# Attention and a two-product MLP in one kernel: reordering the start of the software pipeline

## The chip, the cores and the metric

The kernel runs on one core of a Trainium2 chip. The metric is the device time of one execution in microseconds. The kernel before was run 13 times: the median is 257.85 us, the runs lie between 256.0 and 263.9 us. One execution was recorded by the hardware profiler; its own time is 257.47 us.

The engines are named as in the profile: PE is TensorE (PEld its weight loads), DVE is VectorE, ACT is ScalarE, POOL is GpSimd, SP is SyncE. POOL, SP and ACT also issue DMA transfers. Each engine works through its instructions in the order in which the program emits them, and waits where an operand isn't there yet.

## The reference

Inputs are q, k and v of shape (4, 8, 768, 64) in float32, and two weight matrices of 512 x 2048 and 2048 x 512. Attention is causal with a scale of 1/8. Of the eight heads, 0, 2 and 6 ("retrieval" heads) see all earlier tokens; the others ("stream" heads) see the first four tokens (the sink) and a window of the last 64:

```python
in_win = (rel >= 0) & (rel < int(window))
stream_keep = causal & (is_sink | in_win)
mask = np.where(retr[0, :, 0, 0, None, None], full_mask, stream_mask)
...
a = a / (np.sum(a, axis=-1, keepdims=True) + 1e-09)
attn_out = np.matmul(a, v)
```

The result is laid out as 3072 tokens of 512 features, and then

```python
h = x @ w_in
g = np.maximum(0.01 * h, h)
return (g @ w_out).astype(np.float32)
```

## The kernel before

**Chunks.** The tokens are cut into eight chunks of 384 (`CH`), two for each of the four batches: chunk n is half n % 2 of batch n // 2. For each chunk there are three pieces of work: attention n, product 1 of n (`in_slots`, x times w_in, sixteen ticks of four matmuls and one Prelu on ACT), and product 2 of n (`out_slots`, sixteen parts, 48 matmuls). Each is a list of Python closures; `run` emits a list, `merge` interleaves two lists evenly. The order in which the closures run is the program order of every engine. There is no planner; the order is written out by hand at the bottom of the kernel (lines 517 to 581).

**The steady state.** From chunk 2 on, the stage of chunk n interleaves product 1 of n, product 2 of n - 1 and attention n + 1 (lines 567 to 581). Before that, attention 0 runs alone, then product 1 of chunk 0 with the preparation of chunk 1 between its last ticks, then attention 1 merged with the last two ticks and product 2 of chunk 0 (line 557), then products 1 and 2 of chunk 1 merged with attention 2 (line 564).

**Loads.** `load(n)` issues the K, Q and V transfers of chunk n on POOL, in that order, three or six transfers each, with the cast to bf16 in the transfer. From chunk 2 on, K goes into one of two zero-padded buffers `kz[n % 2]` (line 86); the zeros between the heads are written once, by `zeros_k` on DVE (line 136). The weights w_in and w_out are loaded on POOL too, in quarters, between the loads of chunks 0, 1 and 2.

**K and Q transposed.** Attention needs K and Q with the features on the partitions. For chunk 0 `prep_first` and for chunk 1 `prep_pair` do it with PE transposes through PSUM. From chunk 2 on `prep_dma(n)` issues six DMA transposes on SP (lines 236 and 238): K and Q in turn, for each third of the chunk. A score of the first head needs all three thirds of Q.

**V shifted by half a tile.** The window of a stream head spans two tiles of 64 tokens, so V is needed a second time shifted by 64 rows, in `vb`. `v_shift(n)` makes it with two DMA copies (lines 182 and 183), on ACT's queue unless another is given; it must wait for chunk n's V. For chunk 0 `v_shift_pe` does it with matmuls.

**Sinks.** `sink_keys` copies the first four keys of the stream heads to `ksink` on DVE; `sink_values(b)` writes the first four value rows to `vs`, whose last column holds ones for the softmax sum.

**Attention in slots.** A unit is one score group (scores on PE, exp on ACT, mask on DVE), and its product with V follows `LAG` slots later. When both heads of a pair are done, `finish` adds the sinks and normalises on DVE (lines 413 and 415), and `XLAG` slots later `x_t` transposes the result on PE (line 421) and ACT copies it into `xt`, the input of product 1.

**PSUM.** Eight banks are shared by tag: two "ph" (product 1), two "psS" (scores), two "po" (attention output), one "py" (product 2), one "pt" (transposes). A tile of a tag waits until the last user of that bank is done.

**Queues.** The SP order before is: K of chunk 0; V shift 1; transposes of chunk 2; output stores of chunk 0; V shifts 2 and 3; transposes of chunk 3; output stores of chunk 1; transposes of chunks 4 and 5; output stores of chunk 2; and so on. V shifts 4 to 7 are on ACT, at the end of a stage.

Of the kernel before, what the change touches and what calls it, by code (L numbers as in the profile page):

```python
# [21 lines left out]
def kernel(  # L22
# [34 lines left out]
    def bank(tag, shape, dtype):  # L57
        return ps.tile(shape, dtype, name=tag, tag=tag, bufs=BANKS[tag])
# [98 lines left out]
    def late_constants():  # L157

        nc.vector.tensor_copy(shift[:, 0, 0:64], ident[:, 64:128])
        nc.vector.tensor_copy(shift[:, 1, 64:128], ident[:, 0:64])  # L160
        nc.vector.tensor_copy(m_win0[:, 1:], spread(m_w[:], 5, 64))
        nc.vector.tensor_copy(m_win0[:, 0, :], m_caus[:, 0:64])
        nc.vector.memset(m_win0[0:NS, 1, :], 1.0)
        for h in range(H):
            if IS_RETR[h]:
                nc.vector.memset(m_h[:, h : h + 1], 0.0)
        for i in range(2):
            nc.vector.tensor_copy(vs[i][:, :, D], m_h[:])

    def sink_values(b):  # L170
        m = m_h[:, 1:H].rearrange("p (h o) -> p h o", o=1).to_broadcast([128, H - 1, D])
        nc.vector.tensor_tensor(vs[b % 2][:, 1:H, 0:D], spread(sv[:, b, :], H - 1, D), m, op=ALU.mult)

# [25 lines left out]
    def sink_keys(n, p, hh):  # L199
        b, c = divmod(n, 2)  # L200
        h = 2 * p + hh
        if c == 0 and not IS_RETR[h]:
            r = slice(64 * hh, 64 * hh + 64)
            nc.vector.tensor_copy(ksink[b % 2][r, p, NS * h : NS * h + NS], kt[b % 2][r, p, hh, 0:NS])
# [35 lines left out]
    def prep_first():  # L240

        k0 = stage["k"].rearrange("p h (g d) -> p g h d", g=3)
        qts[0] = rot.tile([128, 4, CH], BF16, name="qt", tag="qt", bufs=2)
        nc.vector.tensor_copy(cast["k", 0][:, :, 0:4], k0[:, :, 0:4])
        nc.scalar.activation(out=cast["k", 0][:, :, 4:8], in_=k0[:, :, 4:8], func=ACTF.Copy)
        pts = {}
        for nm, half, tag in (("k", 0, "pt"), ("k", 1, "py"), ("q", 0, "po"), ("q", 1, "po")):
            pt = pts[nm, half] = bank(tag, [128, 2, 4, 128], BF16)
            if nm == "q":
                continue  # L250
            for e in range(2):
                p = 2 * half + e
                for g in range(3):
                    nc.tensor.transpose(pt[:, e, g, :], cast[nm, 0][:, g, 2 * p : 2 * p + 2, :], ident[:])
        for g in range(3):
            for p in range(4):
                nc.tensor.transpose(pts["q", p // 2][:, p % 2, g, :], cast["q", 0][:, g, 2 * p : 2 * p + 2, :], ident[:])
        tok = lambda ap: ap.rearrange("p e (t g) -> p e t g", g=3)

        def k_rows(half, hh, act=False):  # L260
            ps2 = slice(2 * half, 2 * half + 2)
            r = slice(64 * hh, 64 * hh + 64)
            src = pts["k", half][r, :, 0:3, :].rearrange("p e g t -> p e t g")
            dst = tok(kt[0][r, ps2, hh, 0:CH])
            if act:
                nc.scalar.activation(out=dst, in_=src, func=ACTF.Copy)
            else:
                nc.vector.tensor_copy(dst, src)

        def q_rows(half):  # L270
            return (qts[0][:, 2 * half : 2 * half + 2, :].rearrange("p e (g t) -> p e g t", g=3),
                    pts["q", half][:, :, 0:3, :])

        k_rows(0, 0)
        k_rows(0, 1)
        k_rows(1, 0, True)
        k_rows(1, 1)
        late_constants()
        d, r = q_rows(0)
        nc.scalar.activation(out=d, in_=r, func=ACTF.Copy)  # L280
        d, r = q_rows(1)
        nc.vector.tensor_copy(d, r)
        for h in range(H):
            sink_keys(0, h // 2, h % 2)
        sink_values(0)


    xts = {}
    ats_i = [0]

    class Attention:
        def __init__(self, n, score_tags=("psS",), po_tags=("po", "po", "po", "po")):
            self.n = n
            self.b, self.c = divmod(n, 2)
            self.i = self.b % 2
            xts[n] = rot.tile([128, 4, CH], BF16, name="xt", tag="xt", bufs=2)
            self.po = {}
            self.tags = score_tags
            self.po_tags = po_tags
            self.sc = 0  # L300
            self.sink_lo = 128 if self.c == 0 else 0
            self.units = {h: (self.retr(h) if IS_RETR[h] else self.stream(h)) for h in range(H)}
# [118 lines left out]
                nc.tensor.transpose(pt[:, 0, j, :], xs[:, j], ident[:])  # L421
            nc.scalar.activation(out=xts[self.n][:, p, :], in_=pt[:, 0, 0:3, :], func=ACTF.Copy)  # L422

        def slots(self, extra=(), order=range(H), extra_at=None, LAG=2, XLAG=2, sink_after=None):

            extra = list(extra)
            units = []
            seen = set()
            for h in order:
                if seen == (sink_after or {0, 1}) or (2 in seen and h == 1 and not sink_after):  # L430
                    units.append((self.sink, None, None))
                seen.add(h)
                units += self.units[h]
            sink_at = [j for j, u in enumerate(units) if u[1] is None][0]
            last = {p: max([sink_at] + [j for j, u in enumerate(units) if u[2] == p]) for p in range(4)}
            r, box = [], {}
            if extra and extra_at is None:
                r.append(extra.pop(0))
            for t in range(len(units) + LAG + XLAG):
                def slot(t=t):  # L440
                    for p in range(4):
                        if t == last[p] + LAG + XLAG:
                            self.x_t(p, box[p])
                    if t < len(units):
                        units[t][0]()
                    if 0 <= t - LAG < len(units):
                        if units[t - LAG][1]:
                            units[t - LAG][1]()
                        for p in range(4):
                            if t - LAG == last[p]:  # L450
                                box[p] = self.finish(p)
                r.append(slot)
                if extra and t in (extra_at or [last[p] + LAG + XLAG + 1 for p in range(4)]):
                    r.append(extra.pop(0))
            return r + extra
# [2 lines left out]
    gs = {}  # L458
    py = {}

    def in_slots(n):
        def tick(t):
            if t == 0:
                gs[n] = rot.tile([128, NG, CH], BF16, name="g", tag="g", bufs=2)
            ph = bank("ph", [128, 512], FP32)
            for g in range(KG):
                nc.tensor.matmul(ph[:, 0:CH], lhsT=w_in_bf[:, g, 128 * t : 128 * t + 128],  # L467
                                 rhs=xts[n][:, g, :], start=(g == 0), stop=(g == KG - 1))
            nc.scalar.activation(out=gs[n][:, t, :], in_=ph[:, 0:CH], func=ACTF.Prelu, alpha=0.01)  # L469

        return [lambda t=t: tick(t) for t in range(NG)]
# [27 lines left out]
    def run(*lists):  # L499
        for l in lists:  # L500
            for f in l:
                f()
# [32 lines left out]
    for i in range(4):  # L535
        load_w("out", i)
    prep_first()
    a0 = Attention(0, ("psS", "ph")).slots(order=[0, 2, 1, 3, 4, 5, 6, 7], LAG=4, XLAG=3, sink_after={0, 2})
    run(a0[0:8])
    v_shift_pe()  # L540
    run(a0[8:])
    zeros(0, 1)
    nc.vector.memset(ksink[1][:], 0.0)
    zeros_k(0)
    zeros_k(1)
    load(2)
    in0 = in_slots(0)
    run(in0[0:10])
    for p in range(4):
        prep_pair(1, p, ("py", "pt")[p % 2])  # L550
        run(in0[10 + p : 11 + p])
    v_shift(1, nc.sync)
    prep_dma(2)
    load(3)

    a1 = Attention(1, po_tags=("po", "po", "po", "ph")).slots(order=[0, 2, 6, 1, 3, 4, 5, 7])
    run(merge(in0[14:] + out_slots(0), a1))
    v_shift(2, nc.sync)
    v_shift(3, nc.sync)
    load(4)  # L560
    prep_dma(3)
    for h in range(H):
        sink_keys(2, h // 2, h % 2)
    run(merge(in_slots(1) + out_slots(1, ("py", "ph", "py")), Attention(2).slots()))
# [2 lines left out]
    for n in range(2, NCH):  # L567
        a = []
        if n + 3 < NCH:
            load(n + 3)  # L570
        if n + 2 < NCH:
            prep_dma(n + 2)
        if n + 1 < NCH:
            a = Attention(n + 1).slots()
        run(merge(merge(in_slots(n), outs) if outs else in_slots(n), a))
        if n + 2 < NCH:
            v_shift(n + 2)
            for h in range(H):
                sink_keys(n + 2, h // 2, h % 2)
        outs = out_slots(n) if n + 1 < NCH else out_slots(n, ("psS", "psS", "py"), True)  # L580
# [36 lines left out]
```

## Time and profile before

| what | us |
|---|---|
| median of 13 runs | 257.85 |
| profiled execution, its own time | 257.47 |
| span of the profile, first to last instruction | 255.8 |
| PE busy | 228.1 |
| ACT busy | 137.4 |
| DVE busy | 86.8 |
| POOL busy | 80.4 |
| first matmul of product 1, chunk 0 | 20.7 |
| first matmul of product 1, chunk 1 | 58.3 |
| first score of attention 3 | 91.0 |

The profile is a page and a trace that answers questions. The page gives the busy time of each engine, and the span in 40 slices with a digit for the busy tenths; the row PEclk is the clock that TensorE was granted. The waits list who stood still for whom: in total, how many times, the longest. The chain of waits is followed back from the last instruction, at each step to what released it. The timeline gives instructions in order of time (start, length, engine, line, what was written from what), with the idle time before them and what ended it in brackets. A table of stretches gives the busy time of each engine between two moments, with instruction counts in brackets. "DMA qt<-qb" is the transfer that writes `qt` from `qb`; a row of SPq or POOL with DMA in it is the issue of a transfer, not its landing.

### The profile page before, as it was taken

What the parts mean: (1) busy time and instruction counts of PE and PEld (TensorE: products, weight loads), DVE (VectorE), ACT (ScalarE), POOL (GpSimd) and SP (SyncE); (2) the same over time, 40 slices, a digit from 0 to 9 for tenths busy, and PEclk for the clock granted to TensorE, in tenths of its full rate; (3) what the DMA queues carried; (4) which work ended last, traced back from release to release, by engine and by line L of the source; (5) the groups of instructions that cost most, each with busy time, mean ns of one, the idle gap of its engine ahead of it and who ended that gap; (6) DMA issues with size and microseconds to landing.
All of it is one profiled execution on the core that took longest, in us unless ns stands there. A gap on an engine that the chain in (4) does not pass through costs nothing.

```text
span 255.8 us, 5001 instructions
## 1 busy us (share of the span) xinstructions
PE 228.1 (89%) x1984; PEld 137.9 (54%) x2012; DVE 86.8 (34%) x248; ACT 137.4 (54%) x297; POOL 80.4 (31%) x109
## 2 busy tenths in 40 slices
PE   1778866982999999998999999999999999999994
PEld 0464543561566556654665566655665566555543
DVE  6986331272123423333342224333431242211111
ACT  3575463541585279854665676665656577433300
POOL 8983824965491375286640000000000000000000
PEclk9999999997699999999999999999999999999999
DMA  9999999999999999999993971097103100111012
GB/s 161 114 205 179 168 233 174 125 142 172 214 155 141 134 212 160 149 135 177 176 168 71 117 148 44 0 147 163 44 0 107 41 11 32 41 42 43 8 74 85
DMA packets 110971, 30.14 MB, mean 118 GB/s; under 512 B 101732, under 2 KB 107108, under 8 KB 110948
## 3 DMA queue, kind: packets, MB, share of 16 engines
q0 software_dynamic: 76272, 13.24, 71.5%
q1 hardware_dynamic: 33936, 15.23, 32.6%
q10 hardware_dynamic: 740, 1.35, 2.6%
q8 instruction: 16, 0.26, 0.5%
q14 instruction: 7, 0.06, 0.1%
HBM read 27.28 MB, written 6.29 MB: 131 GB/s over the span
## 4 chain that ended last, share of the span: by engine, by line
PE 57%; DMA 28%; POOL 6%; SPq 4%; issue 2%; DVE 1%; ACT 0%; POOLq 0%
PE ph L467 23%; PE py L480 20%; DMA w_out_bf<-in_moe_w_out_dram 6%; DMA qt<-qb 6%; DMA w_in_bf<-in_moe_w_in_dram 5%; PE po L309 4%; PE psS L342 4%; PE psS L480 3%; DMA kz<-in_k_dram 3%; DMA va<-in_v_dram 3%; DMA vb<-va 3%; DMA kt<-kz 3%; SPq L236 3%; POOL va L93 2%; PE psS L378 1%
## 5 line engine op out<-in xcount | busy, mean ns | idle before, releaser
L467 PE MATMUL ph<-xt,w_in_bf 128*128 128x384 bf16 x512 | 103.9, 330 | 0.1
L469 ACT ACTIVATE g<-ph 128x384 bf16<-128x384 f32 x128 | 62.9, 491 | 49.1 <-PE ph L467 48.5
L480 PE MATMUL py<-w_out_bf,g 128*128 128x512 bf16 (+1 forms) x310 | 83.1, 373 | 5.7 <-DMA w_out_bf<-in_moe_w_out_dram 3.8
L467 PEld LDWEIGHTS <-w_in_bf 128*128 128x128 bf16 x512 | 45.6, 98 | 27.6 <-issue 2.8
L480 PEld LDWEIGHTS <-g 128*128 128x128 bf16 x400 | 36.4, 97 | 32.2 <-issue 5.4
L347 ACT ACTIVATE at<-psS 128x384 bf16<-128x384 f32 x81 | 38.6, 491 | 23.4 <-PE psS L342 19.7
L86 POOL DMA_DIRECT2D kz<-in_k_dram x36 | 27.0, 763 | 34.0 <-DMA kt<-kz 20.0
L342 PE MATMUL psS<-qt,kt 128*128 128x384 bf16 (+2 forms) x104 | 26.6, 299 | 4.9 <-DMA qt<-qb 4.7
L485 DVE COPY o<-py 128x512 f32<-128x512 f32 (+1 forms) x21 | 14.3, 679 | 39.6 <-PE py L480 37.6
L93 POOL DMA_DIRECT2D qb<-in_q_dram x24 | 21.3, 902 | 8.2 <-DMA w_out_bf<-in_moe_w_out_dram 1.9
L93 POOL DMA_DIRECT2D va<-in_v_dram x24 | 21.2, 907 | 7.2 <-DMA w_in_bf<-in_moe_w_in_dram 4.6
L422 ACT ACTIVATE xt<-pt 128x384 bf16<-128x384 bf16 x32 | 15.7, 489 | 14.5 <-PE pt L421 14.0
L383 ACT ACTIVATE ats<-psS 128x384 bf16<-128x384 f32 x38 | 18.5, 494 | 8.1 <-PE psS L378 8.1
L353 DVE TENSOR_TENSOR at<-at,m_caus 128x128 bf16<-128x128 bf16 x24 | 5.4, 224 | 50.7 <-ACT at L347 50.6
L309 PE MATMUL po<-va,at 128*128 128x65 bf16 x237 | 20.2, 195 | 0.2 <-DVE at L353 0.2
L309 PEld LDWEIGHTS <-at 128*128 128x128 bf16 x252 | 16.2, 99 | 5.8 <-DVE at L353 0.7
L342 PEld LDWEIGHTS <-kt 128*128 128x128 bf16 x108 | 10.5, 101 | 15.3 <-issue 7.9
L415 DVE TENSOR_TENSOR xs<-po,linv 128x384 bf16<-128x384 f32 x31 | 17.3, 557 | 1.1
L378 PEld LDWEIGHTS <-kt 128*128 128x128 bf16 x240 | 12.0, 99 | 6.2 <-issue 0.5
L309 PEld LDWEIGHTS <-ats 128*128 128x128 bf16 x240 | 11.8, 97 | 6.1 <-DMA vb<-va 1.3
L309 PE MATMUL po<-va,ats 128*128 128x65 bf16 x137 | 13.2, 194 | 0.5 <-DVE xs L415 0.4
L421 PE MATMUL pt<-ident,xs 128*128 128x128 bf16 x96 | 10.6, 219 | 3.2 <-DVE xs L415 2.0
(90 smaller groups left out, 157.7 us busy)
## 6 DMA issues: line engine op xcount, KB each, us to landing
out_dram<-o SPq DMA_DIRECT2D x23, 256.0 KB, 2.3
qb<-in_q_dram POOLq DMA_DIRECT2D x24, 128.0 KB, 6.7
va<-in_v_dram POOLq DMA_DIRECT2D x24, 128.0 KB, 8.0
kz<-in_k_dram POOLq DMA_DIRECT2D x36, 64.0 KB, 8.4
w_in_bf<-in_moe_w_in_dram POOLq DMA_DIRECT2D x4, 512.0 KB, 8.1
w_out_bf<-in_moe_w_out_dram POOLq DMA_DIRECT2D x4, 512.0 KB, 12.1
vb<-va SPq DMA_DIRECT2D x4, 195.0 KB, 6.9
vb<-va ACTq DMA_DIRECT2D x4, 195.0 KB, 3.1
```

Source lines behind the costliest of these rows:

```text
L86: nc.gpsimd.dma_start(out=kz[n % 2][:, g, hh::2, D * hh : D * hh + D], in_=nat[nm][b, c, :, hh::2, g])
L93: nc.gpsimd.dma_start(out=o, in_=nat[nm][b, c, :, :, g])
L309: nc.tensor.matmul(o, lhsT=lhsT, rhs=rhs, start=first, stop=False, skip_group_check=True)
L342: nc.tensor.matmul(s[:, off : off + w], lhsT=kt[i][:, p, hh, 128 * kj : 128 * kj + 128], rhs=qts[n][:, p, lo:CH], start=(j == 0), stop=(j ...
L347: nc.scalar.activation(out=a[:, 0:off], in_=s[:, 0:off], func=ACTF.Exp, scale=SM)
L378: nc.tensor.matmul(s[:, 64 * m : 64 * m + 64], lhsT=kt[i][:, p, hh, k0 : k0 + 128], rhs=qts[n][:, p, 64 * m : 64 * m + 64], start=(m == 0) ...
L383: nc.scalar.activation(out=av_, in_=s[:, 0:CH].rearrange("p (j e f) -> p j e f", j=3, e=2), func=ACTF.Exp, scale=SM)
L415: nc.vector.tensor_tensor(xs[:], po[:, :, :, 0:D], linv.to_broadcast([128, 3, 2, D]), op=ALU.mult)
L422: nc.scalar.activation(out=xts[self.n][:, p, :], in_=pt[:, 0, 0:3, :], func=ACTF.Copy)
L467: nc.tensor.matmul(ph[:, 0:CH], lhsT=w_in_bf[:, g, 128 * t : 128 * t + 128], rhs=xts[n][:, g, :], start=(g == 0), stop=(g == KG - 1))
L469: nc.scalar.activation(out=gs[n][:, t, :], in_=ph[:, 0:CH], func=ACTF.Prelu, alpha=0.01)
L480: nc.tensor.matmul(py[n][:, 0 : c1 - c0], lhsT=gs[n][:, ng, 128 * tt : 128 * tt + 128], rhs=w_out_bf[:, ng, c0:c1], start=(ng == 0), stop= ...
```

## The change

- Attention 1 is split: its first eight slots are merged with the last five ticks of product 1 of chunk 0, the rest with product 2 of chunk 0. For that the preparation of chunk 1 moves from behind tick 10 to behind tick 7.
- Product 1 of chunk 0 takes its PSUM banks in turn from "ph" and "psS".
- `zeros_k(1)` moves from before the load of chunk 2 to behind attention 1, and V shift 2 and `load(3)` follow it there. Since `load(3)` writes K into `kz[1]`, it waits for these memsets.
- On SP the transposes of chunk 3 now stand ahead of V shift 3.
- V shifts 4 to 7 go to SP, each directly behind the transposes of the same chunk, instead of to ACT at the end of the stage.
- `XLAG` is 3 instead of 2 by default. Attention 0 takes two banks in turn for the transposes of its result.
- In the first attention, `sink_keys` stands ahead of the constants, `sink_values(0)` behind the first six slots, the PE shift of V two slots earlier, and the ones column of `vs` is written by `sink_values` for each batch.

```diff
@@ sink_values, prep_first
-        for i in range(2):
-            nc.vector.tensor_copy(vs[i][:, :, D], m_h[:])
     def sink_values(b):
+        nc.vector.tensor_copy(vs[b % 2][:, :, D], m_h[:])
...
+        for h in range(H):
+            sink_keys(0, h // 2, h % 2)
         late_constants()
...
-        for h in range(H):
-            sink_keys(0, h // 2, h % 2)
-        sink_values(0)
@@ Attention
-        def __init__(self, n, score_tags=("psS",), po_tags=("po", "po", "po", "po")):
+        def __init__(self, n, score_tags=("psS",), po_tags=("po", "po", "po", "po"), x_tags=("pt",)):
-        def slots(self, extra=(), order=range(H), extra_at=None, LAG=2, XLAG=2, sink_after=None):
+        def slots(self, extra=(), order=range(H), extra_at=None, LAG=2, XLAG=3, sink_after=None):
-                            self.x_t(p, box[p])
+                            self.x_t(p, box[p], self.x_tags[p % len(self.x_tags)])
@@ in_slots
-            ph = bank("ph", [128, 512], FP32)
+            ph = bank(tags[t % len(tags)], [128, 512], FP32)
@@ the order of the work
-    a0 = Attention(0, ("psS", "ph")).slots(order=[0, 2, 1, 3, 4, 5, 6, 7], LAG=4, XLAG=3, sink_after={0, 2})
-    run(a0[0:8])
+    a0 = Attention(0, ("psS", "ph"), x_tags=("pt", "py")).slots(order=[0, 2, 1, 3, 4, 5, 6, 7], LAG=4, XLAG=3, sink_after={0, 2})
+    run(a0[0:6])
+    sink_values(0)
     v_shift_pe()
-    run(a0[8:])
+    run(a0[6:])
     zeros(0, 1)
     nc.vector.memset(ksink[1][:], 0.0)
     zeros_k(0)
-    zeros_k(1)
     load(2)
-    in0 = in_slots(0)
-    run(in0[0:10])
+    in0 = in_slots(0, ("ph", "psS"))
+    run(in0[0:7])
     for p in range(4):
         prep_pair(1, p, ("py", "pt")[p % 2])
-        run(in0[10 + p : 11 + p])
+        run(in0[7 + p : 8 + p])
     v_shift(1, nc.sync)
     prep_dma(2)
+    a1 = Attention(1, po_tags=("po", "po", "po", "ph")).slots(order=[0, 2, 6, 1, 3, 4, 5, 7])
+    run(merge(in0[11:], a1[:8]) + merge(out_slots(0), a1[8:]))
+    zeros_k(1)
+    v_shift(2, nc.sync)
     load(3)
-    a1 = Attention(1, po_tags=("po", "po", "po", "ph")).slots(order=[0, 2, 6, 1, 3, 4, 5, 7])
-    run(merge(in0[14:] + out_slots(0), a1))
-    v_shift(2, nc.sync)
-    v_shift(3, nc.sync)
     load(4)
     prep_dma(3)
+    v_shift(3, nc.sync)
...
             prep_dma(n + 2)
+            v_shift(n + 2, nc.sync)
...
         if n + 2 < NCH:
-            v_shift(n + 2)
```

More of the change, by code (lines that the diff above doesn't have):

```diff
@@ L299, in __init__ @@
             self.po_tags = po_tags
+            self.x_tags = x_tags
             self.sc = 0
@@ L459, with in_slots @@
     py = {}
-    def in_slots(n):
+    def in_slots(n, tags=("ph",)):
         def tick(t):
```

## The prediction

> **What bounds the kernel now.** I read the page first, then the waits of TensorE, then the stretches and the timeline around the longest of them.
>
> ```profile
> span 255.8 us, 5001 instructions
> PE 228.1 (89%) x1984; PEld 137.9 (54%) x2012; DVE 86.8 (34%) x248; ACT 137.4 (54%) x297; POOL 80.4 (31%) x109
> PEclk9999999997699999999999999999999999999999
> ```
>
> TensorE is the bound: 27.7 us of the span are not PE time, and the clock dips once, near 60 us. The waits of PE (in total, times, longest) say where it stands still:
>
> ```profile
> PE psS L342 <- DMA qt<-qb: 4.7, 1, 4.7
> PE py L480 <- DMA w_out_bf<-in_moe_w_out_dram: 3.8, 3, 1.9
> PE po L309 <- DMA vb<-va: 1.1, 1, 1.1
> PE py L214 <- DMA qb<-in_q_dram: 0.6, 1, 0.6
> ```
>
> The largest single one is attention 2's first score (L342), which needs the last transposed Q of chunk 2. The table of stretches (first column us, then PE, PEld, DVE, ACT, POOL, PEclk, DMA, GB/s) shows what it costs:
>
> ```profile
> 58.26:63.75 5.49, 0.81 (x6) 0.32 (x5) 1.33 (x6) 0.75 (x2) 3.45 (x5) 0.78 1.68 185
> 63.75:68.17 4.42, 4.42 (x15) 2.12 (x16) 0.52 (x2) 1.85 (x4) 0.75 (x2) 0.50 1.75 249
> 68.17:91.04 22.87, 22.57 (x203) 13.48 (x204) 7.60 (x21) 12.21 (x27) 11.15 (x14) 1.00 1.97 152
> ```
>
> 4.68 us of standstill and then 4.42 us at half clock, another 2.2 us of work lost. Why the transpose was late is in the timeline:
>
> ```profile
> 48.13 3.76 POOL L86 DMA_DIRECT2D kz<-in_k_dram  x5
> 54.09 1.76 POOL L93 DMA_DIRECT2D qb<-in_q_dram  x2 [1.12 <-DMA va<-in_v_dram]
> 55.06 1.33 SPq L238 DMA_TRANSPOSE qt<-qb  x1
> ...
> 59.61 0.47 SPq L182 DMA_DIRECT2D vb<-va  x1
> ...
> 71.17 0.46 SPq L182 DMA_DIRECT2D vb<-va  x1
> 72.29 0.46 SPq L183 DMA_DIRECT2D vb<-va  x1
> 72.85 1.79 SPq L236 DMA_TRANSPOSE kt<-kz  x1
> ```
>
> The last transpose of chunk 2 is issued at 55.06 and in the chain of waits lands 8.55 us later, while POOL has chunk 3's K loads (48.13) and Q loads (54.09) in flight. Six transposes with no load beside them take 12.2 us from first issue to last landing (138.69 to 150.86, the last one 2.9 us); here they take 19.5. Chunk 3's own transposes wait on SP until 72.85, behind the V shift of chunk 3 (71.17), which waits for the V load.
>
> **The change, part by part.** The sum is made against the profiled execution: 257.47 us, 1.7 around a span of 255.8; it lies 0.4 under the median of 257.85.
>
> *Prologue.* Sink keys ahead of the constants, `sink_values(0)` after six slots, a second bank for the X transposes, four banks for product 1: DVE work is reordered ahead of the first mask (sink values cost 0.63 us, the two ones-column copies 0.40), and gaps of 0.21, 0.44, 0.40 and 0.88 us before product 1 shrink. I estimate product 1 starting about 0.8 us earlier than 20.71. I cost this at nothing: all of it ends at w_out, whose last quarter lands at 43.1 (28.57 plus 14.5), whatever PE does; the POOL order before it does not change. Without that cover it would be a gain of 0.8. The per-batch ones copy (about 0.2 us of DVE, three times) hides beside 15 us of ACT and PE work per stage; uncovered it costs 0.6.
>
> *Preps of chunk 1 after seven ticks instead of ten.* This puts a wait on PE. K of chunk 1 lands at 24.6, 25.5 and 26.5 (issue 12.65, 13.53, 14.39 plus 11.9 to 12.1), the last Q at 29.1 (17.93 plus 11.2), and PE would be there at 19.9 + 7 x 0.67 = 24.6. So it drips transposes until 29.2, with all of PE's stream queued behind:
>
> ```profile
> 29.19 0.23 PE L214 MATMUL py<-ident,qb 128*128 128x128 bf16 x1 [0.63 <-DMA qb<-in_q_dram]
> ```
>
> Afterwards three more ticks (1.95 us) and four more attention slots (four scores and their products, 1.0) have to fit before w_out's last quarter. From 29.2 to 43.15 PE was busy 10.14 of 13.95 us, so 3.8 are free and 2.95 are used. Net: 1.0 us of attention 1 moves ahead of 43.15, and the stage's end goes from 58.26 to about 57.0 (XLAG 3 gives the other 0.2; the 0.58 wait for the single X bank at 57.66 stays).
>
> [...] In the trace the clock halved about 2.3 us after the last matmul (0.78 over 5.49 us is 2.4 us at half). [...] By the row of before (clock 1.00 with a 0.76 us wait there) nothing is lost. [...]
>
> *Chunk 3's loads held.* `zeros_k(1)` now stands on DVE behind the last copy of product 2 of chunk 0, and the K loads wait for it; K is first in the load, so Q, V and all later loads on POOL queue behind. No trace shows transposes of chunk 2 without that load. The bounds: the last one lands 2.5 to 6.9 us after its issue in the rows without loads (2.5, 2.9, 3.7, 6.9) and 8.55 in the row of before. V of chunk 2 is down at 54.5 (47.26 plus 7.2), so I take 3.4, near the median of the quiet rows: 55.06 + 3.4 = 58.5. PE is ready at 57.7 after one tick, waits 0.8 us, too short for the clock. **Gain 63.75 - 58.5 = 5.25, plus 2.2 of clock: 7.45 us** (ends: 2.2 and 8.2).
>
> What is late next is chunk 3. First load: 57.0 + 0.9 (output copy) + 0.8 (the two memsets) + 0.2, and the 0.3 from above: 59.2, against 48.13. Six K issues of 0.75 put Q's issue at 63.7, and Q's first third lands 5.7 us later (6.0 for chunk 2's last third, 13.1 in the crowd of before): 69.4. But now the transposes are ahead of the V shift on SP, so the first Q transpose goes at 69.4 instead of 74.75. From that issue to the last landing before took 16.2 us, with loads beside it as there will be: 85.6. Attention 3 began at 91.04 with 0.14 us of waiting; its PE is now ready at 90.9 - 7.45 = 83.45. **Cost: about 2.0 us of standstill** (ends: 0 at the quiet pace, 10 us from first Q issue; 12 with the clock if Q lands as late as 13.1). At 2.0 I leave the clock up, close to the limit.
>
> *V shifts on SP.* For chunks 4 to 7 two issues of 0.5 us leave ACT at each stage's end and go right after the transposes on SP. Chunk 4's shift goes at about 96 instead of 112.26, so PE's wait on vb goes: **gain 1.1**. On SP only output stores stand behind; three output buffers cover them, and V has landed long before. Shift 3 now goes at about 80.5 behind transposes; attention 3's first window head needs it 5 us after its start, with some 3 us to spare.
>
> *XLAG 3.* Two waits of the X transposes on DVE in later stages, 0.62 and 0.23: **gain 0.6**.
>
> Sum: 7.45 - 2.0 + 1.1 + 0.6 = 7.15. Span 248.65, run 250.3, against the median **250.7 us**, 2.8% faster. Less than 0.5% (1.3 us) can't be told from no change here.
>
> **Rivals.**
> - *Chunk 3 becomes the new wait and eats the gain.* Place: L342 at the start of attention 3. Without its wait the gain is 9.15; a standstill over about 2.3 us adds 2.2 of half clock, so it breaks even when the last Q transpose lands 6.95 us after 83.45, at 90.4, and is slower beyond 91.7. If Q lands 13.1 us after issue as before: first transpose 76.8, end 93.0, standstill 9.5, time 257.85 - 9.15 + 11.7 = **260.4**. For it: POOL starts 11 us later and the transposes keep meeting loads. Against it: that 13.1 was measured among chunk 2's transposes, which are over. A middle course, landing at 88.5, gives 255.9.
> - *The transposes' own pace holds, not the load.* Chunk 2 lands at 61.5 (6.4 after issue). PE stands 3.8 us, the half clock stays, gain 2.25 + 1.7 and no wait at attention 3: **253.9**. For it: quiet rows up to 6.9. Against: the other three.
> - *The early wait costs a long half clock.* The dip of before lasted 6.8 us; the same after 29.2 loses 3.4, of which 0.85 fit: the stage ends at 59.6, attention 2 at 60.3, with chunk 3 as late relative to it: **252.5**.
>
> **How the numbers follow.** Likeliest 0.55 (its own range 247.5 to 253.5); chunk 3 late 0.28, of which 0.10 still faster, 0.07 level, 0.11 slower; transposes' own pace 0.10; early half clock 0.07. Faster 0.82, same 0.07, slower 0.11. The low end, 247.5, is the likeliest with no wait at chunk 3 and a full 8.2 at chunk 2, less a little; the high end, 257.5, takes in the middle course and leaves the slower case out.
>
> **What would show it.** L342's wait on qt at attention 2 under 1.5 us and no clock under 1.0 between 58 and 68; first K load of chunk 3 at 58 to 60; a PE wait on qb of some 4 us near 25 to 29, possibly with a dip of the clock behind it; attention 3's first score at 83 to 86 behind a wait on qt of 0 to 2.5 us; no PE wait on vb. I am wrong if attention 3 stands still for over 2.5 us with the clock at half, or if attention 2 still begins after 61.

## The result, and the profile after

The changed kernel takes **252.94 us** (median of 11 runs, 250.88 to 254.34) against 257.83 (48 runs of the kernel before): a ratio of **0.981** with a 95% interval of 0.979 to 0.984. A run more than 1.5% above the fastest of its kernel is left out of every ratio here, so a ratio can differ a little from the quotient of the medians. The profiled execution took 252.87 us around a span of 251.2. The time lies inside the range; the step that was to bring most of it did not happen.

The head of the page and the waits of TensorE after the change (in total, times, longest):

```profile
span 251.2 us, 5005 instructions
PE 226.7 (90%) x1986; PEld 137.8 (55%) x2012; DVE 86.7 (35%) x250; ACT 137.1 (55%) x297; POOL 79.8 (32%) x109
PEclk9999999999799999999999999999999999999998
```

```profile
...
PE psS L341 <- DMA qt<-qb: 4.0, 1, 4.0
PE py L213 <- DMA qb<-in_q_dram: 2.0, 3, 0.7
PE py L479 <- DVE o L484: 1.2, 2, 0.7
```

The wait that the change was forecast to remove is still there: attention 2 stands 4.0 us for the last transposed Q of chunk 2, and the clock dips behind it. What is gone are the waits on `w_out_bf` and on `vb`; what is new is the drip on `qb` at line 213, which was forecast at some 4 us and is 2.0. The stretches around attention 2 (us, then PE, PEld, DVE, ACT, POOL, PEclk, DMA, GB/s) answer to those of before:

```profile
57.62:62.45 4.83, 0.81 (x5) 0.32 (x4) 2.48 (x8) 0.75 (x2) 3.33 (x5) 0.95 1.61 191
62.45:65.35 2.90, 2.90 (x10) 1.35 (x11) 0.23 (x1) 0.98 (x2) 1.47 (x2) 0.50 1.29 299
65.35:88.00 22.65, 22.55 (x204) 13.73 (x205) 7.66 (x22) 12.53 (x28) 11.20 (x14) 1.00 1.97 156
```

Why the transpose is still late is in the timeline. The row with L86 is the K load of chunk 3, and the two rows with MEMSET are `zeros_k(1)`, for which that load was supposed to wait:

```profile
47.63 4.50 POOL L86 DMA_DIRECT2D kz<-in_k_dram  x6
...
53.83 0.87 POOL L93 DMA_DIRECT2D qb<-in_q_dram  x1 [0.60 <-DMA va<-in_v_dram]
```

```profile
53.76 2.34 SPq L237 DMA_TRANSPOSE qt<-qb  x1
...
58.54 0.38 DVE L137 MEMSET kz<- 128x384 uint32 x1
58.95 0.38 DVE L138 MEMSET kz<- 128x384 uint32 x1
...
60.25 1.84 SPq L235 DMA_TRANSPOSE kt<-kz  x1
```

The load goes at 47.63, 10.9 us *ahead* of the memsets, half a microsecond earlier than before the change. **Nothing holds it.** `zeros_k` writes the halves of `kz[1]` that stay zero, line 86 writes the halves that hold a head: they share a buffer but not a byte, so neither waits for the other. My description of the change said that the load "waits for these memsets". That sentence is wrong, and I had taken it over from the order of the calls without looking at which columns each of them writes. The last transpose, issued at 53.76, again lands 8.55 us later, as in the chain of before:

```profile
53.76 8.55 DMA qt<-qb
```

What the change did bring can be read from the moment at which each attention's first score starts (us):

| attention | 2 | 3 | 4 | 5 | end of span |
|---|---|---|---|---|---|
| before | 63.75 | 91.04 | 112.00 | 138.92 | 255.8 |
| before, another execution (c_before) | 63.12 | 91.15 | 112.11 | 139.28 | 256.1 |
| after | 62.45 | 88.69 | 108.70 | 134.31 | 251.2 |

Against the first row, 1.3 us are gained by attention 2, another 1.0 by attention 3 (a shorter half clock, 3.41 instead of 6.83 us, and no wait), 1.0 by attention 4 and 1.3 by attention 5, and nothing later.

### The profile page after: what moved, and what is told of

Its sections match the earlier page's. It is cut to its first block, busy times and chain, and to the rows that moved or that the text cites. A ratio compares the mean times of both kernels' runs of the same rounds, so it can differ in the third digit from the quotient of the medians.

```text
span 251.2 us, 5005 instructions
## 1 busy us (share of the span) xinstructions
PE 226.7 (90%) x1986; PEld 137.8 (55%) x2012; DVE 86.7 (35%) x250; ACT 137.1 (55%) x297; POOL 79.8 (32%) x109
## 4 chain that ended last, share of the span: by engine, by line
PE 76%; DMA 11%; POOL 3%; SPq 3%; ACT 2%; issue 2%; DVE 1%; POOLq 0%
PE ph L466 29%; PE py L479 25%; PE po L308 6%; PE psS L341 5%; DMA qb<-in_q_dram 4%; PE psS L479 3%; DMA qt<-qb 3%; DMA w_in_bf<-in_moe_w_in_dram 3%; PE psS L377 2%; SPq L235 2%; PE pt L420 2%; PE ph L479 1%; PE psS L321 1%; PE psS L466 1%; POOL va L93 1%
## 5 line engine op out<-in xcount | busy, mean ns | idle before, releaser
L466 PE MATMUL ph<-xt,w_in_bf 128*128 128x384 bf16 x480 | 97.9, 329 | 0.1
L468 ACT ACTIVATE g<-ph 128x384 bf16<-128x384 f32 x120 | 59.0, 492 | 49.5 <-PE ph L466 49.0
L479 PEld LDWEIGHTS <-g 128*128 128x128 bf16 x400 | 35.7, 97 | 28.6 <-issue 2.9
L346 ACT ACTIVATE at<-psS 128x384 bf16<-128x384 f32 x81 | 39.2, 492 | 17.2 <-PE psS L341 16.1
L86 POOL DMA_DIRECT2D kz<-in_k_dram x36 | 26.9, 765 | 29.7 <-DMA kt<-kz 12.1
L484 DVE COPY o<-py 128x512 f32<-128x512 f32 (+1 forms) x21 | 14.2, 677 | 40.4 <-PE py L479 38.3
L93 POOL DMA_DIRECT2D qb<-in_q_dram x24 | 21.3, 896 | 14.5 <-DMA va<-in_v_dram 6.8
L421 ACT ACTIVATE xt<-pt 128x384 bf16<-128x384 bf16 x30 | 14.7, 489 | 11.2 <-PE pt L420 10.7
L350 DVE TENSOR_TENSOR at<-at,m_caus 128x256 bf16<-128x256 bf16 x24 | 7.0, 291 | 25.7 <-ACT at L346 25.7
```

The costliest lines, as they stand in the source:

```text
L86: nc.gpsimd.dma_start(out=kz[n % 2][:, g, hh::2, D * hh : D * hh + D], in_=nat[nm][b, c, :, hh::2, g])
L93: nc.gpsimd.dma_start(out=o, in_=nat[nm][b, c, :, :, g])
L346: nc.scalar.activation(out=a[:, 0:off], in_=s[:, 0:off], func=ACTF.Exp, scale=SM)
L479: nc.tensor.matmul(py[n][:, 0 : c1 - c0], lhsT=gs[n][:, ng, 128 * tt : 128 * tt + 128], rhs=w_out_bf[:, ng, c0:c1], start=(ng == 0), stop= ...
```

## The experiments

### The hold made real: x1_held

One column of a head's half is written by DVE behind attention 1. The K load overwrites it, so now the two really meet in one byte; the result is not touched.

```diff
     zeros_k(1)
+    nc.vector.memset(kz[1][:, 0, 0, 0:1], 0.0)
     v_shift(2, nc.sync)
     load(3)
```

> The changed kernel plus one memset of a single column of chunk 3's K buffer behind attention 1; that column is one that the first K transfer writes, so the load now has to wait. In the changed kernel the first K transfer of chunk 3 went out at 47.6 us, as before the change: theory A says that the zeros and the K load never touch the same bytes, so nothing was held. Theory A expects here: first K transfer of chunk 3 at 58 to 60; attention 2's first score at 58.4 to 59.5 instead of 62.45, no half clock (gain 3.5 + 1.4); then attention 3 waits 1 to 3 us for chunk 3, whose last transpose lands at about 85.5 with PE ready at 83.5. Sum 2 to 4 us less than the changed kernel: 249 to 251. Rival 1, the transposes' own pace: attention 2 still begins after 61, time 252.5 to 255. Rival 2, chunk 3 eats the gain: attention 3 stands still for 5 us or more with the clock at half, 254 or more.

Measured: **249.85 us** (247.93 to 253.38, 6 runs), ratio 0.970 (0.965 to 0.974). POOL's timeline, and behind it two stretches of PE:

```profile
59.81 4.46 POOL L86 DMA_DIRECT2D kz<-in_k_dram  x6 [11.83 <-DVE kz L557]
64.21 2.70 POOL L93 DMA_DIRECT2D qb<-in_q_dram  x3
```

```profile
58.40:83.45 25.05, 25.04 (x221) 14.98 (x219) 9.59 (x32) 14.25 (x32) 21.67 (x27) 1.00 2.13 143
83.45:85.07 1.62, 0.01 (x1) 0.01 (x1) 0.69 (x1) 0.09 (x1) 0.00 (x0) 1.00 1.59 199
```

The bracket is the proof of the hold: 11.83 us of POOL standing still, ended by DVE's write in line 557. Attention 2 begins at 58.40 and PE is busy for 25.04 of the next 25.05 us at full clock; then attention 3 stands 1.62 us for Q of chunk 3. This is the forecast's picture, row by row, in a kernel that is one instruction away from the change.

### A hold from another place: z1_held_qt

The same column, written by POOL from the last column of chunk 2's transposed Q, so that the load goes as soon as the transposes are down instead of when attention 1 is over.

```diff
     zeros_k(1)
+    nc.gpsimd.tensor_copy(kz[1][:, 0, 0, 0:1], qts[2][:, 0, CH - 1 : CH])
     v_shift(2, nc.sync)
```

> The changed kernel with a hold that ends with chunk 2's last Q transpose: one column copied on POOL from that tile into the K buffer ahead of the load. Theory A: K of chunk 3 goes out at 56.5 to 57.5 instead of 59.8, attention 2 still begins at 58.4, chunk 3 lands 2 to 3 us earlier and attention 3's wait of 1.6 us is gone: 248 to 249. Rival: POOL's copy is slow or the earlier load meets the output stores, and the time stays at 249.5 to 250.5.

Measured: 250.56 us (248.22 to 253.16, 6 runs), ratio 0.971 (0.964 to 0.977), no better than x1_held. The load went at 58.30, 1.5 us earlier, but the first third of Q landed at 71.6 instead of about 70.0: output stores of chunk 0 and V shift 2 were now in flight beside it, but that they held it up was not tried. The wait at attention 3 was 1.2 us. This profile shows something else, in the preparation of chunk 1 and right behind it (same columns as above):

```profile
26.41:29.82 3.41, 1.18 (x8) 0.56 (x7) 0.11 (x1) 0.49 (x1) 3.00 (x5) 1.00 2.43 155
29.82:33.23 3.41, 3.41 (x21) 2.31 (x19) 2.02 (x6) 0.98 (x2) 2.63 (x4) 0.50 1.43 198
```

PE is busy for 1.18 of 3.41 us while it drips transposes (it does a few whenever a piece of Q lands), and then runs 3.41 us at half clock. The profiles of the change (clock 1.00 from 20.0 to 57.6) and of x1_held (1.00 from 27 to 33) have the same drip and no dip behind it: it comes in some executions and not in others. The last section sets such stretches side by side.

### The split of attention 1: x4_nosplit, y1_held_nosplit, z3_split10

x4_nosplit undoes the split in the changed kernel, y1_held_nosplit does the same in x1_held (so it has the real hold):

```diff
-    in0 = in_slots(0, ("ph", "psS"))
-    run(in0[0:7])
+    in0 = in_slots(0)
+    run(in0[0:10])
...
-        run(in0[7 + p : 8 + p])
+        run(in0[10 + p : 11 + p])
...
-    run(merge(in0[11:], a1[:8]) + merge(out_slots(0), a1[8:]))
+    run(merge(in0[14:] + out_slots(0), a1))
```

> The changed kernel with the split undone: preparation of chunk 1 behind tick 10, two banks for product 1, attention 1 merged with the last two ticks and product 2 as before. Theory A: attention 2 is released by chunk 2's last transpose (62.45) while PE was ready at 58.4, so the split gains nothing: within 0.5 us of the changed kernel, 252.5 to 253.5. Rival: the 1.3 us by which attention 2 began earlier come from the split; 254 to 255.

> The kernel with the real hold, split undone. Theory A: with the hold attention 2 begins when PE gets there (58.4, no wait), so now the split counts: attention 1 ends about 1.0 to 1.2 us later, attention 2 begins at 59.4 to 59.8, and the held load moves back as much; 250.5 to 251.3 against 249.85 with the split. Rival: the split is worth nothing here either, within 0.3 us of 249.85.

Measured: x4_nosplit 252.45 us (251.88 to 253.84, 6 runs), ratio 0.983 (0.979 to 0.987); y1_held_nosplit 249.94 us (249.67 to 250.53, 6 runs), ratio 0.972 (0.967 to 0.976). Neither can be told from its partner with the split (252.94 and 249.85). Without the hold this is plain: attention 2 waits for the transposes whenever PE arrives. With the hold it isn't: in the profiles attention 2 starts at 58.4 with the split and at 59.8 without. But the mean clock of the six runs of y1_held_nosplit was 0.997 to 1.0, while x1_held had three runs at 0.999 or above (247.9 to 249.5 us) and three at 0.986 to 0.993 (250.2 to 253.4). By my estimate one dip of 3.41 us at half clock, in a span of 247.8, takes 0.007 off the mean clock of such a run and costs 1.7 us, so these three had one or two. The split's gain is given back by the clock in half of the runs.

z3_split10 keeps the hold and the split, and moves the preparation back behind tick 10, where Q of chunk 1 has landed when PE gets there. Product 1 of chunk 0 is back on two banks with it, so the four banks were not tried alone:

```diff
-    in0 = in_slots(0, ("ph", "psS"))
-    run(in0[0:7])
+    in0 = in_slots(0)
+    run(in0[0:10])
...
-        run(in0[7 + p : 8 + p])
+        run(in0[10 + p : 11 + p])
...
-    run(merge(in0[11:], a1[:8]) + merge(out_slots(0), a1[8:]))
+    run(merge(in0[14:], a1[:8]) + merge(out_slots(0), a1[8:]))
```

> The kernel with the real hold and the split, but with chunk 1's preparation behind tick 10 as before the change, so that TensorE doesn't drip transposes from 25.8 to 29.2. Theory B: in the split kernel the drip lets the clock halve for 3.4 us in some executions (the profile with the hold ended by the transposes shows 0.5 from 29.8 on; three of six runs with the hold have a mean clock of 0.986 to 0.993, without the split all six have 0.997 to 1.0). Then here every run has a clock of 0.997 or more, attention 2 begins at 58 to 58.6 and the time is 248 to 249.3, with under 1.5 us between the runs. Rival: the runs with a lower clock stay, so the drip isn't their cause.

Measured: **248.72 us** (248.05 to 248.97, 6 runs), ratio **0.965** (0.960 to 0.969), the clock at 0.999 to 1.0 in every run. Attention 2 starts at 57.7, attention 3 at 84.1. Its waits:

```profile
PE psS L341 <- DMA qt<-qb: 1.6, 2, 1.4
...
PE py L479 <- DMA w_out_bf<-in_moe_w_out_dram: 1.1, 1, 1.1
```

The drip is gone and PE waits for `w_out_bf` again. So the split is worth about 1.2 us (249.94 - 248.72; the ranges of the runs don't overlap), and the preparation behind tick 7 costs about 1.1 (249.85 - 248.72). The second figure is nearly all clock: the three runs of x1_held without a dip have a median of 249.07, 0.35 above z3_split10, and their range overlaps its own. These runs were not made side by side; the kernel before, run beside each group, had medians 0.7 us apart. This version is the fastest apart from z5_both and z6_lag2 below, which can't be told from it.

### The hold with the old order on SP: y2_hold_only

The kernel before with a real hold alone. V shift 3 stays ahead of chunk 3's transposes on SP, as it was.

```diff
-    load(3)
...
     run(merge(in0[14:] + out_slots(0), a1))
+    nc.vector.memset(kz[1][:, 0, 0, 0:1], 0.0)
     v_shift(2, nc.sync)
+    load(3)
     v_shift(3, nc.sync)
```

> The kernel before with one part alone: chunk 3's load really held behind attention 1 (its memset covers a column that the K load writes), but with V shift 3 still ahead of chunk 3's transposes on SP. Theory A: attention 2 begins at about 59 without a half clock (gain 6.5 to 7), but the transposes of chunk 3 wait for V of chunk 3 (lands at about 75), their last one lands at 92 or later, PE is ready at about 84 and stands still for 7 us or more with the clock at half: 258 to 261, no gain or a loss. Rival: the hold alone carries the gain, 250 to 252, and the order on SP does not matter.

Measured: **264.56 us** (262.84 to 265.67, 6 runs), ratio 1.029 (1.023 to 1.034), slower than before and than both cases expected. SP's timeline, the two largest waits of PE, and the stretches at attention 3:

```profile
72.12 0.46 SPq L182 DMA_DIRECT2D vb<-va  x1
...
73.64 1.56 SPq L236 DMA_TRANSPOSE kt<-kz  x1
...
87.10 1.40 SPq L238 DMA_TRANSPOSE qt<-qb  x1
```

```profile
PE psS L342 <- DMA qt<-qb: 9.2, 1, 9.2
PE po L309 <- DMA vb<-va: 2.7, 1, 2.7
```

```profile
84.00:93.30 9.30, 0.07 (x2) 0.01 (x1) 0.69 (x1) 0.16 (x1) 2.23 (x4) 0.63 1.65 163
93.30:96.70 3.40, 3.40 (x14) 1.71 (x15) 0.00 (x0) 1.75 (x4) 3.29 (x5) 0.50 1.42 262
```

Attention 2 begins at 59.1 without a wait, so the hold does its part. But V shift 3 waits for the held V, the transposes wait behind it on SP until 73.64, and attention 3 begins at 93.3 after 9.2 us. That is the place of the rival in which chunk 3 becomes the new wait, and its numbers (landing at 93.0, standstill 9.5) come out almost as forecast, but by luck: it had the first Q transpose wait for Q until 76.8 and 16.2 us from there, where it now went at 75.30 and 18.0 us passed. With the transposes behind the V shift, the hold costs more than it gains.

### V shifts on SP, XLAG 3: x2_shift, x3_lag, z6_lag2

```diff
@@ x2_shift, on the kernel before
             prep_dma(n + 2)
+            v_shift(n + 2, nc.sync)
...
         if n + 2 < NCH:
-            v_shift(n + 2)
@@ x3_lag, on the kernel before
-        def slots(self, extra=(), order=range(H), extra_at=None, LAG=2, XLAG=2, sink_after=None):
+        def slots(self, extra=(), order=range(H), extra_at=None, LAG=2, XLAG=3, sink_after=None):
@@ z6_lag2, on z3_split10
-        def slots(self, extra=(), order=range(H), extra_at=None, LAG=2, XLAG=3, sink_after=None):
+        def slots(self, extra=(), order=range(H), extra_at=None, LAG=2, XLAG=2, sink_after=None):
```

> The kernel before with one part alone: V shifts 4 to 7 on SP behind the transposes of the same chunk. Prediction's step: PE's wait on vb of 1.1 us near 120 goes, 256.7, nothing else moves. Rival: the shift on SP delays the stores or the transposes of chunk 5 and the gain is under 0.3 us.

> The kernel before with one part alone: XLAG 3 by default. Prediction's step: 0.6 us from two waits on DVE (0.62 and 0.23), 257.2. Rival: no difference beyond 0.2 us, since the wait on vb behind them takes up what is gained.

> The best kernel so far (real hold, split, preparation behind tick 10) with XLAG back at 2: what XLAG 3 is worth where neither the half clock nor the wait on vb can blur it. The prediction's step says 0.6 us, from the two waits of the X transposes on DVE (0.62 and 0.23): 249.3 to 249.7 against 248.72. The run with XLAG 3 alone in the kernel before gained 2.1 us in the medians. If the step was mis-sized in itself: 250.3 or more here. If that 2.1 came mostly from the wait on vb, which also vanished in that run, and from the clock: 249.3 to 249.7.

Measured: x2_shift 256.07 us (22 runs), ratio **0.995** (0.993 to 0.997), which is 1.3 us; x3_lag 255.66 us (22 runs), ratio **0.991** (0.988 to 0.994), which is 2.4 us; z6_lag2 248.59 us (6 runs), ratio 0.966 (0.961 to 0.971), not to be told from z3_split10.

The V shift is simple: no wait on `vb` is left in x2_shift, and from attention 4 to 5 its profile has 25.6 us instead of 26.9. XLAG isn't. The stage from attention 3 to 4 is 0.7 us shorter with XLAG 3 on the kernel before (20.27 against 20.96) and 0.6 on z3_split10 (20.34 against 20.93). On the kernel before, the ratio shows three times as much, and most of it is the wait on `vb`: it is gone there too, though the shift is still on ACT, and from attention 4 to 5 the profile again has 25.6 us. The second issue of that shift starts at 110.08, when attention 4 starts, and takes 0.55 us; before it started at 112.26, 0.3 us behind that, and took 1.41. So x2_shift and x3_lag remove the same wait, and their gains can't be added. On z3_split10 the medians show nothing, although the stage shows the 0.6: with XLAG 2, attention 3 started 0.8 us earlier (83.3 against 84.1), with a shorter wait. Whether that was the execution or XLAG stays open.

### The kernel before, once more: c_before

The kernel before unchanged, recorded a second time, to see how much of the difference in starts is the execution's own.

> The kernel before once more, for a second profile: how far attention 2's first score and the length of the half clock wander between executions of one program. Theory A: both wander, 62.0 to 63.8 and 3.4 or 6.8 us, so that the 1.3 us by which attention 2 began earlier in the changed kernel are not its doing. Rival: 63.7 and 6.8 again.

Measured: 257.85 us, span 256.1. Its starts are in the table above: attention 2 is 0.6 us earlier than in the first profile, with a half clock of 3.4 instead of 6.8 us, and attention 3 then waits 1.36 us (0.14 in the first), so that both executions are level from attention 3 on. Half of the 1.3 us at attention 2 and the shorter dip can therefore not be credited to the change.

### K transposed ahead of Q: z4_kfirst, z5_both

For chunks 2 and 3 all K transposes go ahead of the Q transposes on SP, in y1_held_nosplit (z4_kfirst) and in z3_split10 (z5_both). In x1_held the first K transpose goes at 63.51 and the first Q transpose, for want of Q, only at 70.09, with the other K transposes behind it.

```diff
-        for g in range(3):
+        steps = [(e, g) for g in range(3) for e in "kq"]
+        if n < 4:
+            steps = [(e, g) for e in "kq" for g in range(3)]
+        for e, g in steps:
```

> Real hold, no split, and for chunks 2 and 3 the three K transposes on SP ahead of the three of Q. Theory: SP stood idle from 65 to 71 waiting for the first third of Q while all of K was there; K first fills this, chunk 3's last Q transpose is issued 2.5 us earlier, and attention 3's wait of 1.3 us goes: 248.3 to 249.0 against 249.94. Rival: the transposes are bound by the DMA engines, not by their issue, and the wait stays: 249.7 to 250.2.

> Hold, split with the preparation behind tick 10, and K first, together. If both steps hold: attention 2 at 57.5 to 58.5, no wait at attention 3, no half clock before the end: 246.5 to 248. If the K-first step falls: as z3.

Measured: z4_kfirst 249.65 us (248.96 to 250.28, 6 runs), ratio 0.969 (0.963 to 0.974); z5_both 248.74 us (248.02 to 249.31, 6 runs), ratio 0.965 (0.961 to 0.970). Neither can be told from its base. SP's timeline in z4_kfirst, and PE's wait on Q there:

```profile
64.26 7.21 SPq L241 DMA_TRANSPOSE kt<-kz  x3
71.57 5.64 SPq L239 DMA_TRANSPOSE qt<-qb  x3
```

```profile
PE psS L346 <- DMA qt<-qb: 1.7, 2, 1.5
```

The wait at attention 3 nearly goes, as meant (84.4, a standstill of 0.2), and 1.5 us appear at attention 4 (106.1), whose transposes now come that much too late. In z5_both 0.7 us appear there (104.5). The wait is worth nothing while the next one stands behind it.

## Why the prediction was right, and where it was wrong

That the time lies in the range is luck in the main. The range is 10 us wide, and its upper end lies 0.3 us under the median of the kernel before; the case that was given 0.55 did not occur, and the gain came from terms that were forecast small or at nothing.

**The hold.** "The K loads wait for it" failed. It was the premise of the largest term (7.45 less 2.0), and it was not among the rivals: I listed none in which the change doesn't do what it says. By the forecast's own test ("if attention 2 still begins after 61") it was wrong. Lines 86, 137 and 138 say which columns they write; I took a write of zeros and a write of data into one tile for the same bytes.

**The mechanism behind the hold** was right, as x1_held shows in a kernel with the hold made real: first K load at 59.8 (forecast 59.2), attention 2 at 58.4 (58.5), first third of Q landed at about 70.0 (69.4), PE ready for attention 3 at 83.45 (83.45), a wait of 1.6 us (2.0), 249.85 us (250.7). The 3.4 us that I took for the last transpose of chunk 2 without loads beside it lies among those measured: at most 2.6 in z3_split10 (issued at 55.07, attention 2 starts at 57.7 without a wait on it), 3.9 in z1_held_qt (53.91, POOL's wait for it ends at 57.8), 5.5 in z5_both (53.22, attention 2 waits for it until 58.75).

**What took its place.** Without the hold, the forecast's remaining terms are 1.1 and 0.6, or 1.7 us; measured were 4.9 (4.6 between the two profiles). Of the 4.6, 2.3 lie behind the start of attention 3: these are the two small terms, 0.7 in the stage of XLAG and 1.3 with the wait on `vb`. The other 2.3 lie before it. Chunk 3's transposes run from 60.25, not 72.85, because V shift 3 is behind them, so attention 3 no longer waits. In the kernel before that wait is 0.1 us when attention 2 is late and 1.4 when it is earlier (c_before), so that attention 3 starts at 91.0 to 91.2 either way. Most of the rest is that attention 2 starts 0.7 to 1.3 us earlier; how much of this is the change, and how much the execution, is open. The new order on SP was not run alone.

**Preparation behind tick 7.** The stage's end was forecast at 57.0 and came at 57.62, a gain of 0.6 instead of 1.2. The step that was off is "all of it ends at w_out": PE has no wait on `w_out_bf` any more, so the cover was used up, and the prologue that I had costed at nothing because of it did not start product 1 earlier: it starts at 20.97, and at 20.71 and 21.67 in the two executions of the kernel before. With the hold and without the drip the split brought the 1.2.

**The clock behind the drip.** The row of before (clock 1.00 with a wait there) spoke for no loss, and it held in the profiles of the change and of x1_held. z1_held_qt shows 3.41 us at half clock after the drip all the same, and this is not hidden once attention 2 no longer waits: about 1.1 us in the medians. The 0.3 us "from above" in the start of chunk 3's load (59.2) is a term that no run shows: in the change that load went at 47.63, and in x1_held, where it was held, at 59.81 with the clock at 1.00 behind the drip. My measure for the clock, a standstill of over 2.3 us, was the wrong one: it went by the length of a wait, and the clock fell 3.51 us into the standstill in the change, and 1.6 us into it in x3_lag.

**The other terms.** V shifts on SP: 1.1 forecast, 1.3 measured, the wait on `vb` gone. XLAG: 0.6 forecast, 0.6 to 0.7 in its stage, the medians undecided.

**The rivals.** The one for the slower side did not occur in the change, which held nothing; in y2_hold_only its place was right, its numbers by luck. The one that came nearest is the transposes' own pace, with 253.9 us, a standstill of 3.8 (4.0 measured) and the half clock. Its reason is wrong all the same: with chunk 3's loads really held, attention 2 starts at 58.4, so it was the loads and not the pace.

## What to carry to other kernels

Where a change relies on one operation waiting for another, look up the bytes that both write or read before costing what follows; here a shared tile was not yet a dependency (the load went at 47.63, the memsets at 58.54), and one shared column made it one (POOL stood 11.83 us in x1_held). A load that is held back is paid for by everything that queues behind it (in y2_hold_only V shift 3 went at 72.12, and chunk 3's transposes from 73.64), so move the consumers that don't need it ahead first: a hold gained 1.2% on the changed kernel and cost 2.9% on the kernel before, where two DMA issues on SP stand ahead of the transposes. A new wait of PE costs more than its length if the clock falls behind it (in y2_hold_only 3.40 us at half clock behind 9.2 us of standstill), so a slightly later place without a wait (here three ticks) can be the better one; and a profile with the clock up does not show that the next execution keeps it (x1_held: 1.0 in the profiled run, 0.986 to 0.993 in three of the other five).

## What was not expected of the hardware

**The clock did not go by the length of a wait.** It fell 2.28 us into the standstill ahead of attention 2 before the change (59.07 to 61.35), 3.51 us into it after the change (58.43 to 61.94), and 1.6 us into it in x3_lag; the whole 1.62 us of standstill in x1_held ran at 1.00, and so did the longest wait on `w_out_bf` in before, 1.87 us. What the traces of before and after do show is a step: but for the last, at the end of the span, the stretches of one clock that they record are whole multiples of 3.413 us long, in the kernel before 47.79, 6.83 and 187.73 us (14, 2 and 55 times that), after the change 47.79, 3.41 and 184.32 (14, 1 and 54 times). Cut into windows of this length, the traces show this (columns as above; before at two places, c_before and x1_held):

```profile
37.45:40.87 3.42, 1.60 (x10) 0.76 (x10) 0.00 (x0) 0.49 (x1) 0.74 (x1) 1.00 1.24 208
40.87:44.28 3.41, 2.59 (x26) 1.47 (x24) 0.29 (x2) 1.36 (x3) 1.36 (x2) 1.00 2.19 158
```

```profile
57.93:61.35 3.42, 1.14 (x8) 0.39 (x4) 1.33 (x6) 0.98 (x2) 1.21 (x2) 1.00 1.68 145
61.35:64.76 3.41, 1.01 (x4) 0.53 (x5) 0.00 (x0) 0.49 (x1) 2.91 (x4) 0.50 1.46 255
64.76:68.17 3.41, 3.41 (x13) 1.62 (x12) 0.52 (x2) 1.36 (x3) 0.07 (x1) 0.50 1.90 226
```

```profile
59.95:63.36 3.41, 0.24 (x2) 0.21 (x3) 0.46 (x1) 0.00 (x0) 2.67 (x4) 1.00 1.74 202
63.36:66.77 3.41, 3.41 (x14) 1.66 (x13) 0.23 (x1) 1.76 (x4) 0.90 (x2) 0.50 1.52 279
```

```profile
24.13:27.54 3.41, 2.03 (x14) 1.12 (x12) 0.00 (x0) 1.63 (x4) 3.24 (x4) 1.00 2.43 155
27.54:30.95 3.41, 2.09 (x18) 1.31 (x18) 1.42 (x5) 0.49 (x1) 2.67 (x5) 1.00 2.16 166
```

In before the window with 1.14 us of PE work was followed by one at half clock, the one with 1.60 was not. PE still stood for most of the first half-clock window (1.01 us of work), and the next one ran at half too; in c_before a window with 0.24 was followed by half clock, the first half-clock window was full (3.41), and the dip is half as long. The drip of x1_held falls into two windows with 2.03 and 2.09 us of work each, and no dip follows; in z1_held_qt one window has 1.18, and one does. The windows lay differently against the same program in the two executions (an edge at 61.35 in before, at 59.95 and 63.36 in c_before), and the dip was 6.83 us long in the one and 3.41 in the other. In the windows shown, full clock was followed by half behind 0.24, 1.14 and 1.18 us of PE work, and by full clock behind 1.60, 2.03 and 2.09. Why, and where between them it turns, was not shown; no run was made to test it.

**Transposes took longer beside loads, and a load took longer beside transposes.** From the first issue to the last landing, the six transposes of chunk 2 took 19.5 us before and 18.7 after the change (43.63 to 62.3), with chunk 3's loads in flight; with the loads held they took at most 14.2 (43.54 to 57.7 in z3_split10), 13.7 (z1_held_qt) and 14.5 (z5_both). In the other direction, the first third of chunk 3's Q took 11.6 us to land in the change (52.33 to 63.9), beside the transposes of chunk 2, and 5.8 in x1_held (64.21 to 70.0), behind them. An earlier issue did not bring an earlier landing: in z1_held_qt K was issued 1.5 us earlier than in x1_held (58.30 against 59.81), and the first third of Q landed 1.6 us later (71.6 against 70.0).
